# Inverses of pairs two and three of chunks on GpSimd, and a new cost model for the planner that orders the instructions

## The chip, the cores and the metric

One core of one Trainium2 chip. The metric is the time of one execution of the program on the device, in microseconds (us). Engines are named as the profile names them: PE (TensorE), DVE (VectorE), ACT (ScalarE), POOL (GpSimd), SP (SyncE, which here issues nearly all transfers).

## What is computed

A recurrent attention with a matrix state per head, over 768 positions, and then two feed-forward layers over the same 3072 tokens:

```python
batch, n_heads, seq, head_dim = (4, 8, 768, 40)
for t in range(S):
    y[:, :, t] = np.einsum('bhd,bhde->bhe', rt, state)
    Sa = np.einsum('bhde,bhe->bhd', state, at)
    state_decay = state * wt[:, :, None, :] - np.einsum('bhd,bhe->bhde', Sa, bt)
    state = state_decay + np.einsum('bhd,bhe->bhde', vt, kt)
x = y.transpose(0, 2, 1, 3).reshape(3072, 320)
h = x @ w_in;  g = h * np.tanh(log1p(exp(h)));  x = g @ w_out       # layer 1, d_ff 2048
h = x @ w_in2; g = h * np.cos(h);               out = g @ w_out2     # layer 2, d_ff 2048
```

## The kernel before

**Attention by chunks.** The 32 heads (batch times heads) are split into two halves of 16, the 768 positions into 24 pieces of 32. A *chunk* g = 0 to 47 is one piece of one half, g = 2c + half. For each chunk, `pre(g)` loads its inputs (line 565), scans the decays (571 to 577), scales a, k and b (585, 591), clears the other halves of the AM tile on POOL (memsets, 599), multiplies (PE, 608; transposes 641), masks the result (DVE, 618) and writes a 32 x 32 triangular matrix per head to `l_d` in DRAM (631, 632). `inverse(bt)` takes a *pair* of chunks, batch bt = chunks 2bt and 2bt+1: it loads their triangular matrices into XM (668), inverts the two 16 x 16 diagonal blocks of each by 14 rounds of a multiply (683) and an add (681), each depending on the one before, sets the diagonal by a memset (690), stores to `t_d` (694) and loads back as TT (698). `halves(bt)` then fills in the off-diagonal block (DVE 725, PE 720, DVE 728, PE 722, copy on ACT or DVE). `chain(g)` is the serial part: the right-hand side from the state (PE 791, copied by ACT, 797), its product with the inverse (805, for the first four chunks also 814), products 863 and 889, the new state (DVE 900, PE 933) and the output y (DVE 908). Chunk g needs the state of chunk g - 2.

**Feed-forward.** A block is 256 tokens, which are four chunks: block 0 needs chunks 0 to 3, block 1 chunks 4 to 7, and so on. `layer1(blk)` loads its input (1045 to 1047), splits it into a high and a low part (ACT 1050, DVE 1052), and multiplies (PE 993, 974) with nonlinear work between (ACT 1066, 1068, DVE 1071). `prep` brings the weights in 25 tiles for layer 1: load (458), convert (ACT 465, DVE 470 and 475, ACT or DVE 396/398), low half on POOL (505). `layer2` is similar with wider tiles (PE 1008 and 1025, POOL 1154).

**What sets the order.** All of this is put into tasks (`P.add(engine, duration, function, preds, ...)`), and `Plan.run` simulates the machine to list them: it takes, again and again, the engine and task that could start first, by the tasks' predicted durations, hops between engines, buffer rings, a port shared by DVE and POOL (`port=True`), and, for PE, a model of its clock (`HOT`, `DENSE` and each task's `cols`) and of the cost to change tile shapes. Among tasks that can start alike the lower `prio` goes first: chains about -1e4, `pre(g)` -5e3 + 10g, an inverse -5e3 + 10(g0 + 2) - 32, the weights of layer 1 -4921, the feed-forward blocks from 0 up. The functions are called in the order found, and that is the instruction order of every engine and of SP's queue; on the chip the engines run it as it stands, with semaphores. A transfer is a task of SP with a fixed time in the queue (0.5 to 2.0) and a fixed latency (`DMA_LAT` = 3.0, and up to 1.5 more) before its users may start. `TIE` seeds a change of up to 1% of each predicted duration.

Inverses: in `inverse`, `own = bt >= 3` decides whether the rounds run on POOL or, for the first three batches, on DVE.

Of the kernel before, what the change touches and what calls it, by code (L numbers as in the profile page):

```python
# [20 lines left out]
S = 768  # L21
# [34 lines left out]
class Task:  # L56
    __slots__ = ("eng", "dur", "fn", "preds", "acq", "rel", "aset", "lat", "prio", "end", "n_wait", "succ", "ready", "cols", "engs", "takes", "name", "durs", "bias", "ffn", "port", "mode", "soft", "pull", "mate")
# [24 lines left out]
HOT = 2750.0  # L82
# [6 lines left out]
SP_SAFE = 1.0  # L89
# [9 lines left out]
class Plan:  # L99
# [23 lines left out]
    def run(self):  # L123
# [15 lines left out]
        tick, hot, count, tick_no = TICK, False, 0.0, 0  # L139
        order = {id(t): i for i, t in enumerate(self.tasks)}  # L140
        while done < len(self.tasks):
# [67 lines left out]
            if e == "PE":  # L209
# [27 lines left out]
            for u in t.succ:  # L237
                for x in u.engs:
                    u.ready[x] = max(u.ready[x], free[e] + (HOP.get((e, x), 0.15) if t.lat is None else t.lat))
# [12 lines left out]
def body(ctx, tc, ins, out):  # L252
# [166 lines left out]
    EARLY = 1  # L419
# [4 lines left out]
    am_on, GLE = lambda g, d: ("DVE", 0.385), ("DVE",)  # L424
# [14 lines left out]
    def prep(layer, names, prio, after, stage, stage2, half):  # L439
# [5 lines left out]
        for kind, k, c0, n in jobs(layer):  # L445
# [32 lines left out]
            t3 = P.add("DVE", dve(n, 0.5), cvt1, preds=[t1], prio=prio, port=True)  # L478
# [75 lines left out]
    def pre(g):  # L554
# [38 lines left out]
        t_k = fifo("kb", P.add(*am_on(g, 0.65), kb_f(0), preds=[t_rp], acq=[("KB", k("KB"))], prio=pr, port=True))  # L593
        t_b = P.add(*am_on(g, 0.65), kb_f(1), preds=[t_k, t_a1], rel=[k("RP")] + ([] if g == 1 else [k("IN")]), prio=pr, port=True)
# [6 lines left out]
        t_z0 = P.add("POOL", 0.31, az_f(0), preds=[t_a1], prio=pr)  # L601
        t_z1 = P.add("POOL", 0.31, az_f(1), preds=[t_z0], prio=pr)
# [8 lines left out]
        t_g = P.add("PE", 0.46, g1, preds=[t_z1, t_b], acq=[("PA", k("G"), 4)], cols=925, prio=pr)  # L611
# [31 lines left out]
        def kbe(e):  # L643
            def f(eng):
                kp = pa(k("KT"))[64 * e:64 * e + 64, 0:4 * QP].rearrange("r (q x) -> r q x", x=QP)
                for p in range(2):
# [4 lines left out]
                    cols=500, prio=pr)  # L651
        KBe[g] = [P.add(KBE, 0.4 + 0.2 * e, kbe(e), preds=[t_t], rel=[k("KT")], prio=pr) for e in range(2)]

    def inverse(bt):
# [17 lines left out]
        own = bt >= 3  # L672
# [31 lines left out]
    def halves(bt, t):  # L704
# [22 lines left out]
        t = P.add("PE", HV_P, mm(0), preds=[t], acq=[("PA", k)], cols=180, prio=pr)  # L727
# [3 lines left out]
        t = P.add("PE", HV_P, mm(1), preds=[t], rel=[(k, "s")], cols=180, prio=pr)  # L731
# [41 lines left out]
    def chain(g):  # L773
# [34 lines left out]
        if g < DIRECT:  # L808
# [8 lines left out]
            def ztev(b, p):  # L817
                def f(eng):
# [4 lines left out]
            tz = P.add("PE", 0.3, ztm, preds=[t, ttld[g]], acq=[("PA", k("ZT0"), 2), ("PA", k("ZT1"), 2)], cols=230, prio=pr)  # L823
            zt = [P.add(EITHER, 0.27, ztev(b, p), preds=[tz, io[g][1]], rel=[k(f"ZT{b}")], bias=B_CH, prio=pr)
                  for b in range(2) for p in range(2)]
            t = P.add("PE", 0.3, zmm, preds=[t, tz, ttld[g]], acq=[("PA", k("Z"), 4)],
                      rel=[k("RS"), ("TT", bt)], cols=230, prio=pr)
        else:
            t = P.add("PE", 0.3, zmm, preds=[t, ttld[g]], acq=[("PA", k("Z"), 5)],
                      rel=[k("RS"), ("TT", bt)], cols=230, prio=pr)  # L830
# [8 lines left out]
            t2 = P.add("PE", 0.46, ztm, preds=[tz], acq=[("PA", k("ZT"), 2)], rel=[k("ZS")], cols=1000, prio=pr)  # L839
# [25 lines left out]
        r0 = P.add("PE", 0.46, rvz, preds=zt, acq=[("PA", k("V"), 2)], rel=[k("VR")], cols=925, prio=pr)  # L865
# [12 lines left out]
        for h in range(2):  # L878
            ve[h] = P.add("DVE", 0.41, rve(h), preds=[r0] + z[2 * h:2 * h + 2] + [ve[i] for i in range(h)], rel=[k("V")], prio=pr)
# [33 lines left out]
        f0 = P.add("PE", 0.56, fmm(0), preds=[ve[0]] + fpre[0], acq=[("PA", k("F0"))], cols=975, prio=pr)  # L913
        f1 = P.add("PE", 0.56, fmm(1), preds=[ve[1], f0] + fpre[1], acq=[("PA", k("F1"))], rel=[k("FL"), k("FR")], cols=975, prio=pr)
        mated("f", c, f0)
        sevs, yevs = [], []
        for h, ft in ((0, f0), (1, f1)):
            s = []
            if not last:
                s = [P.add("DVE", 0.315, sev(h, p), preds=[ft, io[nx][2]], prio=pr) for p in range(2)]  # L920
# [3 lines left out]
            yevs.append(P.add("DVE", 0.26, yev(h), preds=[ft] + s + yevs, acq=y_acq, rel=rel, prio=pr + 1))  # L924
        Sev[g] = sevs
        if not last:
            STev[g] = []
            for p in range(2):
# [13 lines left out]
                t = P.add("PE", 0.21, stm, preds=sevs, acq=[("PA", k(f"S{p}"), 2)], rel=[("SV", nx)], cols=185, prio=pr + 2)  # L942
# [19 lines left out]
    def outs(layer, blk, m, key, pr, preds, po, first, last):  # L962

        t = None
        for f in range(2):
            for j in range(2):
# [12 lines left out]
                t = P.add("PE", 0.44, mm, preds=list(preds) + [t], acq=acq, cols=840,  # L979
# [5 lines left out]
    def h_tasks(layer, key, m, pr, preds, xk):  # L985
        t = h_prev[0]
        for f in range(2):
            for part in range(2):
# [7 lines left out]
                t = P.add("PE", 0.48, mm, preds=list(preds) + [t], cols=880, acq=[("PH", (key, "h"))] if first else [],  # L996
# [4 lines left out]
    def h_wide(key, ft, pr, preds, xk, xh_t, xl_t):  # L1001

        t = h_prev[0]
        for part in range(2):
# [5 lines left out]
            t = P.add("PE", 0.91, mm, preds=list(preds) + [t], cols=1760, acq=[("PH", (key, "h"))] if part == 0 else [],  # L1010
# [4 lines left out]
    def outs_wide(ft, key, pr, preds, po):  # L1015
        t, tj = None, []
        for j in range(4):
# [9 lines left out]
            t = P.add("PE", 0.44, mm, preds=list(preds) + [t], acq=[("PO", (po, j))] if ft == 0 else [], cols=840,  # L1027
# [10 lines left out]
    def layer1(blk, wready):  # L1038
        pr0 = blk * 100
        xk = ("x1", blk)  # L1040
        xr = lambda: XR_t[P.at((xk, "xr"))]

        def ld():
# [143 lines left out]
    S_V = P.add("DVE", 2.0, setup_v, prio=-9e5)  # L1187
# [17 lines left out]
    wr1 = prep(1, ("w_in", "w_out"), -4921.0, [W1_AFTER()], ("RW", "H"), ("RL", "RA1"), half1)  # L1205
# [151 lines left out]
```

## Time and profile before

| | us |
|---|---|
| median of 3 runs | 1089.13 |
| lowest, highest | 1087.01, 1095.01 |
| span of the profiled execution | 1089.5 |
| PE busy in the span | 1006.6 (92%) |
| DVE busy | 742.0 (68%) |
| ACT busy | 544.0 (50%) |
| POOL busy | 429.8 (39%) |

The rows further down come from one execution taken by the hardware profiler. The span runs from its first to its last instruction; all starts are us from the span's start. A view by stretches gives for each stretch of time how long each engine was busy, the granted clock of PE (PEclk, 1.00 is full), and the load of the transfers. A view in order of time gives one line for an instruction or for several merged ones: its start, its length, the engine, the line of the kernel, and in square brackets what the engine was idle for before it. The shares over the whole span hide that the program has stages with different limits, so the stretches matter more than the totals.

### The profile page before, as it was taken

What the parts mean: (1) busy time and instruction counts of PE and PEld (TensorE: products, weight loads), DVE (VectorE), ACT (ScalarE), POOL (GpSimd) and SP (SyncE); (2) the same over time, 40 slices, a digit from 0 to 9 for tenths busy, and PEclk for the clock granted to TensorE, in tenths of its full rate; (3) what the DMA queues carried; (4) which work ended last, traced back from release to release, by engine and by line L of the source; (5) the groups of instructions that cost most, each with busy time, mean ns of one, the idle gap of its engine ahead of it and who ended that gap; (6) DMA issues with size and microseconds to landing.
All of it is one profiled execution on the core that took longest, in us unless ns stands there. A gap on an engine that the chain in (4) does not pass through costs nothing.

```text
span 1089.5 us, 36321 instructions
## 1 busy us (share of the span) xinstructions
PE 1006.6 (92%) x14888; PEld 926.8 (85%) x14888; DVE 742.0 (68%) x1652; ACT 544.0 (50%) x1338; POOL 429.8 (39%) x883
## 2 busy tenths in 40 slices
PE   1276899999999999999999999999999999999998
PEld 1265789888889988888998999999999999999997
DVE  8999888787577786678643797446655656565555
ACT  2345875655474655656564544434433434343433
POOL 4217646547344554355420242103333333333332
PEclk9999999999899999999999999999999999999999
DMA  6547665556445565455533543211100202010100
GB/s 206 149 134 231 173 166 145 154 143 170 108 137 160 145 168 127 122 152 151 137 90 100 173 152 96 85 42 35 42 13 1 54 1 54 1 40 1 25 1 25
DMA packets 109078, 111.88 MB, mean 103 GB/s; under 512 B 64112, under 2 KB 88688, under 8 KB 108912
## 3 DMA queue, kind: packets, MB, share of 16 engines
q1 hardware_dynamic: 108592, 109.24, 36.6%
q8 instruction: 117, 1.92, 0.7%
q14 instruction: 49, 0.40, 0.1%
q10 hardware_dynamic: 320, 0.33, 0.1%
HBM read 91.43 MB, written 18.09 MB: 101 GB/s over the span
## 4 chain that ended last, share of the span: by engine, by line
PE 75%; DVE 12%; DMA 5%; issue 4%; ACT 2%; SPq 1%; POOL 1%; DVEq 0%; POOLq 0%; ACTq 0%
PE bank L993 17%; PE bank L974 15%; PE bank L1008 14%; PE bank L1025 13%; PE bank L889 3%; PE bank L608 2%; DVE SV L900 2%; PE bank L863 1%; DMA VR<-in_vR_dram 1%; PE bank L641 1%; PE bank L837 1%; PE bank L791 1%; PE bank L933 1%; PE bank L805 1%; DVE AM L618 1%
## 5 line engine op out<-in xcount | busy, mean ns | idle before, releaser
L1154 POOL TENSOR_TENSOR GL<-H,GH 128x512 fp32r<-128x512 f32 x94 | 121.9, 1298 | 235.7 <-ACT GH L1152 219.1
L683 POOL TENSOR_TENSOR XT<-XM 64x14 f32<-64x14 f32 (+6 forms) x294 | 97.0, 330 | 174.5 <-DMA XM<-l_d 153.7
L396 ACT ACTIVATE FL<-bank 64x160 f32<-64x160 f32 (+1 forms) x375 | 101.4, 295 | 104.5 <-PE bank L641 51.6
L1145 ACT ACTIVATE T<-T,half_pi 128x512 f32<-128x512 f32 x96 | 69.5, 723 | 105.3 <-DVE T L1142 105.3
L1138 DVE TENSOR_SCALAR T<-bank 128x512 f32<-128x512 f32 x96 | 66.4, 692 | 76.7 <-PE bank L1008 63.2
L681 POOL TENSOR_TENSOR XM<-XM,XT 64x14 f32<-64x14 f32 (+6 forms) x294 | 106.0, 360 | 22.3
L1071 DVE TENSOR_TENSOR GL<-H,GH 128x512 fp32r<-128x512 f32 x96 | 70.1, 734 | 65.5 <-ACT GH L1068 63.7
L1147 DVE TENSOR_TENSOR H<-bank,T 128x512 f32<-128x512 f32 x96 | 66.1, 689 | 54.1 <-ACT T L1145 54.1
L1066 ACT ACTIVATE H<-bank 128x512 f32<-128x512 f32 x96 | 57.5, 598 | 87.9 <-PE bank L993 87.0
L1152 ACT ACTIVATE GH<-H 128x512 fp32r<-128x512 f32 x96 | 60.7, 632 | 73.9 <-DVE H L1147 73.9
L993 PE MATMUL bank<-XH,wih 128*128 128x256 f32 x448 | 95.4, 295 | 0.2 <-ACT GH L1068 0.2
L993 PE MATMUL bank<-XH,wil 128*128 128x256 f32 x448 | 89.7, 282 | 0.0
L993 PE MATMUL bank<-XL,wih 128*128 128x256 f32 x448 | 89.5, 282 | 0.0
L608 PE MATMUL bank<-AM,KB 104*64 104x64 f32 x768 | 37.0, 246 | 48.9 <-DVE KB L591 46.8
L618 DVE TENSOR_TENSOR AM<-bank,maskG 64x128 f32<-64x128 f32 x192 | 55.4, 288 | 35.8 <-PE bank L608 26.8
L608 PEld LDWEIGHTS bank<-AM,KB 104*64 104x64 f32 x768 | 30.5, 155 | 53.4 <-issue 35.4
L993 PEld LDWEIGHTS bank<-XH,wih 128*128 128x128 f32 x448 | 70.0, 192 | 2.2 <-ACT GH L1068 0.3
L993 PEld LDWEIGHTS bank<-XL,wih 128*128 128x128 f32 x448 | 69.7, 192 | 0.0
L993 PEld LDWEIGHTS bank<-XH,wil 128*128 128x128 f32 x448 | 69.6, 192 | 0.0
L1142 DVE SCALAR_TENSOR_TENSOR T<-T,bank 128x512 f32<-128x512 f32 x96 | 65.7, 685 | 2.4
L993 PE MATMUL bank<-XH,wix 128*128 128x256 f32 x224 | 67.1, 300 | 0.0
L900 DVE TENSOR_TENSOR SV<-bank,PE 40x160 f32<-40x160 f32 x184 | 58.9, 320 | 7.0 <-PE bank L889 3.8
(179 smaller groups left out, 2931.6 us busy)
## 6 DMA issues: line engine op xcount, KB each, us to landing
VR<-in_vR_dram SPq DMA_DIRECT2D x96, 160.0 KB
IN<-in_inT_dram SPq DMA_DIRECT2D x94, 161.4 KB
FR<-in_rI_dram SPq DMA_DIRECT2D x48, 180.0 KB
FR<-in_vF_dram SPq DMA_DIRECT2D x48, 144.0 KB
RA<-in_w_in_dram SPq DMA_DIRECT2D x12, 512.0 KB
RA<-in_w_out_dram SPq DMA_DIRECT2D x10, 512.0 KB
SV<-in_vS_dram SPq DMA_DIRECT2D x96, 52.0 KB
TMP<-in_w_in_dram SPq DMA_DIRECT2D x9, 512.0 KB
```

The lines of the kernel that those rows point to most:

```text
L396: A.activation(o, i, AF.Copy)
L608: PE.matmul(gp[c0:c0 + 64, q // 2], kb()[:, q].rearrange("p a t -> p (a t)"), am()[0:104, :, q], start=True, stop=True)
L681: IE.tensor_tensor(out=b[:, 0:i, i + 1:16], in0=b[:, 0:i, i + 1:16], in1=tv, op=ALU.add)
L683: IE.tensor_tensor(out=tv, in0=bc(b[:, i:i + 1, i + 1:16], (2 * n, i, w)), in1=bc(b[:, 0:i, i:i + 1], (2 * n, i, w)), op=ALU.mult)
L900: V.tensor_tensor(out=svn[r, p, :, 64 * h:64 * h + D], in0=fp[r, :, C:], in1=bc(pev(h)[r, :, C:C + 1], (40, 4, D)), op=ALU.mult)
L974: PE.matmul(o, l[:, f, tsl], r, start=(first and f == 0 and i == 0), stop=(last and f == 1 and i == 2))
L993: PE.matmul(hp[:, f], pss[i][0], pss[i][1], start=(i == 0), stop=(i == 7))
L1008: PE.matmul(bank[P.at((key, "h"))][:, 0:512], pss[i][0], pss[i][1], start=(i == 0), stop=(i == 7))
L1025: PE.matmul(o, l, r, start=(ft == 0 and i == 0), stop=(ft == NFF - 1 and i == 2))
L1071: gl = P.add(GLE, (dve(512),), lambda eng, Hv=Hv, key=key: EN[eng].tensor_tensor(out=GL_t[P.at((key, "gl"))], in0=Hv(), in1=GH_t[P.at((key ...
L1145: c = P.add("ACT", act(512, False, 1), lambda f=f, Tv=Tv: A.activation(Tv(f), Tv(f), AF.Sin, scale=-TWO_PI, bias=half_pi), preds=[b], aset ...
L1154: gl = P.add(*((VG, (pool(512), dve(512))) if final and quad == 7 else ("POOL", pool(512))), lambda eng, f=f, Hv=Hv, key=key: EN[eng].tens ...
```

## The change

Two kinds of edits. The first moves instructions from one engine to another: the rounds of the inverses of batches 1 and 2 (pairs two and three) go from DVE to POOL, so that only batch 0 is left on DVE. The others change numbers and rules of the planner, and so the order alone: a transfer now takes one of eight lanes in turn, waits in the queue until its lane is free (`ISSUE`, `LANES`), moves its data one after another with a fitted size and latency (`DMAS`), and its users may start 0.8 us (`LAND`) after that; PE's instructions are counted (`CODE`) and a block of 256 that was not fetched ahead in time costs waiting; durations and columns of many tasks are fitted anew; the clock thresholds follow the new columns; the weights of layer 1 go from priority -4921 (after `pre(7)`) to -4946 (after `pre(5)`); the input of block 0 (load, lines 1050 and 1052) goes from 0 to -9.94e3; the wait that a reused buffer cost an SP task, `SP_SAFE`, goes from 1.0 to 0, and the seed from 97 to 117.

```diff
-TIE = 97
+TIE = 117
-DENSE = 4400.0
-HOT = 2750.0
+DENSE = 5240.0
+HOT = 3277.0
-SP_SAFE = 1.0
+SP_SAFE = 0.0
+OWN, W1_PRIO = 1, -4946.0
+LAT_X = 0.0
+ISSUE, GAP_I, LANES, LAND = 0.36, 0.06, 8, 0.8
+DMAS = {"pre.ld": ((0.8, 2.0), (0.8, 2.0)), "pre.ldm": ((0.2, 1.0), (0.2, 1.0)), "inverse.ld": ((0.35, 1.15), (0.35, 1.15)),
...
+CODE = {"pre.g1": 32, "early.uu": 64, "early.<lambda>": 64, "halves.mm.f": 128, "chain.rhs": 64, "chain.zmm": 64,
...
+BLOCK, AHEAD_C, FETCH = 256, 78, 3.5
...
+                at, per = st, dur / t.code
+                for i in range(code, code + t.code):
+                    if i % BLOCK == 0 and i // BLOCK in fetched:
+                        w = max(0.0, fetched[i // BLOCK] - at)
+                        at, dur = at + w, dur + w
...
+            if t.dm:
+                cur = st
+                for size, l0 in t.dm:
+                    cur = max(cur, lanes[nd % LANES]) + ISSUE
+                    srv = max(srv, cur + l0) + size
+                    lanes[nd % LANES], nd = srv, nd + 1
+                    cur += GAP_I
+                dur = cur - st
...
-            t.end = free[e] + (0.2 if t.lat is None else t.lat)
+            t.end = srv + LAND if t.dm else free[e] + (0.2 if t.lat is None else t.lat)
...
-        own = bt >= 3
+        own = bt >= OWN
...
-                t = P.add("POOL" if own else "DVE", 0.1 + 0.0022 * i * (15 - i) if own else 0.165, step(i, add), preds=[t], lat=0.1 if own else 0.04, prio=pr, port=True)
+                t = P.add("POOL" if own else "DVE", 0.1 + 0.0022 * i * (15 - i) if own else 0.22, step(i, add), preds=[t], lat=0.1 if own else 0.04, prio=pr, port=True)
...
+        px = pr0 - 9.94e3 if blk < EARLY else pr0
...
-    wr1 = prep(1, ("w_in", "w_out"), -4921.0, [W1_AFTER()], ("RW", "H"), ("RL", "RA1"), half1)
+    wr1 = prep(1, ("w_in", "w_out"), W1_PRIO, [W1_AFTER()], ("RW", "H"), ("RL", "RA1"), half1)
```

Examples of the refitted numbers: line 585 from 0.385 to 0.43, line 591 from 0.385 to 0.342, line 618 from 0.27 to 0.298, line 900 from 0.315 to 0.34, line 908 from 0.26 to 0.22, line 797 from 0.29 to 0.328, `setup_v` from 2.0 to 4.0, and `cols` of PE tasks up by 2 to 67%, but for `chain.stm`, which goes down from 185 to 160.

## Rows read from the trace of the kernel before

**Rows 1.** Busy time by stretch: stretch, length, engines, granted clock (PEclk), transfers

```profile
core 0: us, PE busy (x) PEld busy (x) DVE busy (x) ACT busy (x) POOL busy (x), PEclk, DMA share, GB/s
0.00:115.00 115.00, 55.73 (x1325) 47.24 (x1326) 105.29 (x303) 47.19 (x133) 42.84 (x102) 1.00 0.62 177
...
140.00:600.00 460.00, 444.66 (x9946) 404.44 (x9943) 321.52 (x846) 268.86 (x797) 213.91 (x628) 0.99 0.53 140
...
800.00:1080.00 280.00, 280.00 (x1570) 253.53 (x1569) 162.96 (x250) 115.43 (x189) 99.95 (x77) 1.00 0.07 17
...
250.00:300.00 50.00, 46.45 (x994) 42.03 (x984) 31.72 (x84) 27.17 (x81) 26.19 (x84) 0.93 0.51 134
```

**Rows 2.** The same view, two stretches of 10 us within the head

```profile
50.00:60.00 10.00, 6.02 (x215) 4.99 (x215) 9.25 (x32) 3.15 (x12) 0.00 (x0) 1.00 0.24 74
...
70.00:80.00 10.00, 7.24 (x131) 6.29 (x132) 8.88 (x35) 4.68 (x14) 0.14 (x1) 1.00 0.60 152
```

**Rows 3.** DVE in order of time (start, length): batch 0, starts of 1 and 2

```profile
38.17 0.17 DVE L681 TENSOR_TENSOR XM<-XM,XT 64x26 f32<-64x26 f32 x1
...
43.70 0.17 DVE L681 TENSOR_TENSOR XM<-XM,XT 64x14 f32<-64x14 f32 x1
...
47.93 0.17 DVE L683 TENSOR_TENSOR XT<-XM 64x14 f32<-64x14 f32 x1
...
71.92 0.17 DVE L683 TENSOR_TENSOR XT<-XM 64x14 f32<-64x14 f32 x1
...
97.55 0.07 DVE L690 MEMSET XM<- 64x16 f32 x1
```

**Rows 4.** POOL in order of time: the first operation and the memset of batch 3

```profile
89.90 0.21 POOL L683 TENSOR_TENSOR XT<-XM 64x14 f32<-64x14 f32 x1 [3.65 <-DMA XM<-l_d]
...
102.72 0.12 POOL L690 MEMSET XM<- 64x16 f32 x1
```

**Rows 5.** ACT, PE, DVE in order of time: chunks 2, 3 to block 0

```profile
76.48 0.30 ACT L797 ACTIVATE RS<-bank 128x160 f32<-128x160 f32 x1
...
85.18 0.76 PE L814 MATMUL bank<-TT,RS 32*40 32x32 f32 x32 [0.40 <-ACT TT L396]
...
99.06 0.29 DVE L908 TENSOR_TENSOR Y<-bank,PE 104x128 f32<-104x128 f32 x1
...
111.07 0.84 ACT L1050 ACTIVATE XH<-XR 128x768 fp32r<-128x768 f32 x1 [2.56 <-DMA XR<-x_d]
...
113.78 0.95 DVE L1052 TENSOR_TENSOR XL<-XR,XH 128x768 fp32r<-128x768 f32 x1
...
114.73 0.78 PE L993 MATMUL bank<-XH,wih 128*128 128x256 f32 x2
```

**Rows 6.** POOL and DVE in order of time: operations that run side by side

```profile
45.91 1.82 POOL L505 TENSOR_TENSOR wol1a<-H,woh1a 128x512 fp32r<-128x512 f32 x1 [6.93 <-ACT woh1a L396]
...
46.61 1.40 DVE L585 TENSOR_TENSOR AM<-IN,PE 40x256 f32<-40x256 f32 x1
...
48.78 0.71 DVE L571 TENSOR_TENSOR_SCAN PE<-IN,D 104x264 f32<-104x264 f32 x1
...
99.21 0.85 POOL L681 TENSOR_TENSOR XM<-XM,XT 64x36 f32<-64x36 f32 x1
...
99.87 0.76 DVE L571 TENSOR_TENSOR_SCAN PE<-IN,D 104x264 f32<-104x264 f32 x1
```

**Rows 7.** SP's queue in order of time: loads of batches 1 and 2

```profile
41.94 0.78 SPq L668 DMA_DIRECT2D XM<-l_d  x2
...
62.24 0.78 SPq L668 DMA_DIRECT2D XM<-l_d  x2
```

**Rows 8.** The chain that ended last, in order of time: a weight tile

```profile
91.53 4.38 DMA RL<-in_w_in_dram
```

**Rows 9.** ACT in order of time: the input of block 2

```profile
211.44 0.84 ACT L1050 ACTIVATE XH<-XR 128x768 fp32r<-128x768 f32 x1 [1.83 <-DMA XR<-x_d]
```

More of the change, by code (lines that the diff above doesn't have):

```diff
@@ L56 @@
 class Task:
-    __slots__ = ("eng", "dur", "fn", "preds", "acq", "rel", "aset", "lat", "prio", "end", "n_wait", "succ", "ready", "cols", "engs", "takes", "name", "durs", "bias", "ffn", "port", "mode", "soft", "pull", "mate")
+    __slots__ = ("eng", "dur", "fn", "preds", "acq", "rel", "aset", "lat", "prio", "end", "n_wait", "succ", "ready", "cols", "engs", "takes", "name", "durs", "bias", "ffn", "port", "mode", "soft", "pull", "mate", "code", "dm")
     def __init__(self, eng, dur, fn, preds=(), acq=(), rel=(), aset=None, lat=None, prio=0.0, cols=0.0, bias=BIAS, port=False):
@@ L76, in __init__ @@
         self.mate = None
-TIE = 97
+        self.code = 64 if self.name == "chain.ztm" and dur < 0.4 else CODE.get(self.name, 8)
+        self.dm = DMAS.get(self.name) if eng == "SP" else None
+        if self.dm and "prep" in self.name and dur < 0.5:
+            self.dm = ((0.9, 1.6),)
+TIE = 117
 TICK = 10.24 / 3
-DENSE = 4400.0
-HOT = 2750.0
+DENSE = 5240.0
+HOT = 3277.0
 MODE = {"pre.g1": "128x64", "chain.rvz": "128x64", "chain.fmm.f": "128x64", "chain.rhs": "128x32",
@@ L88 @@
 WAIT = 8.0
-SP_SAFE = 1.0
+SP_SAFE = 0.0
[3 more added lines that the diff above has]
+DMAS = {"pre.ld": ((0.8, 2.0), (0.8, 2.0)), "pre.ldm": ((0.2, 1.0), (0.2, 1.0)), "inverse.ld": ((0.35, 1.15), (0.35, 1.15)),
+        "inverse.st": ((0.3, 1.0), (0.3, 1.0)), "inverse.<lambda>": ((0.6, 1.45),),
+        "load_step.f1": ((1.14, 1.6), (0.8, 1.3)), "load_step.f2": ((0.8, 2.0), (0.8, 2.0)),
+        "load_step.f3": ((0.24, 1.2), (0.24, 1.2)), "prep.<lambda>": ((1.8, 1.6),), "chain.yst": ((0.46, 1.0), (0.46, 1.0)),
+        "layer1.ld": ((0.5, 1.45),) * 3, "layer1.<lambda>": ((0.35, 1.3),),
+        "layer2.ld": ((0.3, 1.3),) * 4, "layer2.store": ((0.24, 1.3),) * 2}
+CODE = {"pre.g1": 32, "early.uu": 64, "early.<lambda>": 64, "halves.mm.f": 128, "chain.rhs": 64, "chain.zmm": 64,
+        "chain.rvz": 32, "chain.fmm.f": 32, "chain.sel": 20, "outs.mm": 6, "outs_wide.mm": 6}
+BLOCK, AHEAD_C, FETCH = 256, 78, 3.5
 def mode_cost(a, b):
@@ L139, in run @@
         tick, hot, count, tick_no = TICK, False, 0.0, 0
+        code, fetched = 0, {0: 0.0, 1: 0.0}
+        self.starved = 0.0
+        lanes, nd, srv = [0.0] * LANES, 0, 0.0
         order = {id(t): i for i, t in enumerate(self.tasks)}
@@ L225, in run @@
                     count += t.cols
-                recent.append((st + dur, t.cols))
+                at, per = st, dur / t.code
[3 more added lines that the diff above has]
+                        at, dur = at + w, dur + w
+                        self.starved += w
+                    if (i + AHEAD_C) % BLOCK == 0:
+                        b = (i + AHEAD_C) // BLOCK + 1
+                        fetched[b] = max(at, fetched.get(b - 1, 0.0) - FETCH / 2) + FETCH
+                    at += per
+                code += t.code
+                recent.append((st + dur, t.cols))
+            if t.dm:
[6 more added lines that the diff above has]
+                dur = cur - st
             free[e] = st + dur + sw
@@ L238, in run @@
                 for x in u.engs:
-                    u.ready[x] = max(u.ready[x], free[e] + (HOP.get((e, x), 0.15) if t.lat is None else t.lat))
+                    u.ready[x] = max(u.ready[x], t.end if t.dm else free[e] + (HOP.get((e, x), 0.15) if t.lat is None else t.lat) + (LAT_X if x == "PE" != e and not u.ffn else 0.0))
                 u.n_wait -= 1
@@ L878, in chain @@
         for h in range(2):
-            ve[h] = P.add("DVE", 0.41, rve(h), preds=[r0] + z[2 * h:2 * h + 2] + [ve[i] for i in range(h)], rel=[k("V")], prio=pr)
+            ve[h] = P.add("DVE", 0.43, rve(h), preds=[r0] + z[2 * h:2 * h + 2] + [ve[i] for i in range(h)], rel=[k("V")], prio=pr)
         yb, yc = divmod(c, 2)
@@ L919, in chain @@
             if not last:
-                s = [P.add("DVE", 0.315, sev(h, p), preds=[ft, io[nx][2]], prio=pr) for p in range(2)]
+                s = [P.add("DVE", 0.34, sev(h, p), preds=[ft, io[nx][2]], prio=pr) for p in range(2)]
             sevs += s
@@ L995, in h_tasks @@
                 first = f == 0 and part == 0
-                t = P.add("PE", 0.48, mm, preds=list(preds) + [t], cols=880, acq=[("PH", (key, "h"))] if first else [],
+                t = P.add("PE", 0.48, mm, preds=list(preds) + [t], cols=1024, acq=[("PH", (key, "h"))] if first else [],
                           rel=[(xk, "xh"), (xk, "xl")] if (m == 7 and f == 1 and part == 1) else [], prio=pr)
@@ L1008, in mm @@
                     PE.matmul(bank[P.at((key, "h"))][:, 0:512], pss[i][0], pss[i][1], start=(i == 0), stop=(i == 7))
-            t = P.add("PE", 0.91, mm, preds=list(preds) + [t], cols=1760, acq=[("PH", (key, "h"))] if part == 0 else [],
+            t = P.add("PE", 0.91, mm, preds=list(preds) + [t], cols=2048, acq=[("PH", (key, "h"))] if part == 0 else [],
                       rel=[(xk, "xh"), (xk, "xl")] if (ft == NFF - 1 and part == 1) else [], prio=pr)
```

56 lines of the change are left out of this document (28 added, 28 removed).

## The prediction

> **What bounds the kernel now.** Read the stretches by engine first, then the head by engine in order of time.
>
> From 140 to 600 us TensorE is busy 444.66 of 460, and from 800 to 1080 all of 280 [rows 1]; nothing but less TensorE work or a higher clock shortens that. In the first 115 us it is busy 55.73, so 59.3 are idle, and there VectorE is busy 105.29, 92% [rows 1]. Between 50 and 80 us GpSimd does almost nothing (0.00 and 0.14 in the two stretches shown) while VectorE is at 9.25 and 8.88 of 10 [rows 2]. So the program has two parts: a head that VectorE sets, which ends when the first feed-forward matmul (line 993) starts at 114.73 [rows 5], and a rest that TensorE sets. If the head is shorter and the rest stays as dense, the end moves by the same amount.
>
> **The change part by part.**
>
> *Inverses.* With `own = bt >= 1` the operations of lines 681 and 683 of batches 1 and 2 (pairs two and three) and a memset each go from VectorE to GpSimd: 2 x 28 = 56 steps of the inverses. What a step holds of VectorE is best read from batch 0, which ran almost alone: its 25 steps from the one that starts at 38.17 to the one that starts at 43.70 [rows 3] have 24 pitches in 5.53 us, 0.23 each with the gap. Of interleaved steps the latency is partly hidden by other work, so I take 0.225: 56 x 0.225 = 12.6 us of VectorE time that leaves the head, all of it before 97.6 [rows 3].
>
> Is that time on the path? Batch 1 starts on VectorE at 47.93 and batch 2 at 71.92, right behind it, and its memset is at 97.55 [rows 3]: 24.0 and 25.6 us per batch, because the steps take turns with everything else. On GpSimd batch 3 took from 89.90 to 102.72, 12.8 us, at a busy VectorE [rows 4]. Batch 1's load is issued at 41.94 and batch 2's at 62.24 [rows 7], each long before VectorE is through with it. With some 4 us to land (the tile on the chain took 4.38 [rows 8]; an estimate) GpSimd could finish batch 1 at about 46 + 13 = 59 instead of 71.9, batch 2 at about 79 instead of 97.6. Who waits for batch 1: chunks 2 and 3. Their right-hand side is copied by 76.48 + 0.30 = 76.8, and the product with the inverse starts at 85.18 [rows 5]: 8.4 us in which only the inverse is missing. Their last y is at 99.06, and it releases the input of the first feed-forward block [rows 5]. So the direct path gives 8.4 us, and the VectorE budget of the same stretch 12.6; since VectorE has hardly a gap before and behind that bubble, I take 12.6 and keep 8.4 as what is sure of it.
>
> *What it costs GpSimd.* 2 x 12.8 = 25.6 us, laid on an engine idle for most of 40 to 90 [rows 2]: nothing, while that cover lasts. Behind these steps in GpSimd's order stand the memsets of line 599, which the next pair's first matmuls (line 608) need, and the low halves of the weights (line 505). A step of 12.8 / 28 = 0.46 ahead of a memset delays it by that much; only a batch that waits for its own load would hold them for longer.
>
> *Contention.* An operation of VectorE can stand still beside one of GpSimd: line 585 at 46.61 takes 1.40 and ends only when line 505 (45.91 + 1.82 = 47.73) is over [rows 6]. Nothing here shows a step of batch 1 or 2 on GpSimd; the nearest rows are batch 3's. There the step at 99.21 stretched to 0.85 itself, while the scan that VectorE ran behind it took 0.76 against 0.71 at 48.78 [rows 6]. Bounds: nothing, and a whole pitch per step, 56 x 0.46 = 25.8. I take the scan's 0.05: 56 x 0.05 = 2.8 us.
>
> The Trainium skill (SBUF — State Buffer, "Who interferes with whom") says that a VectorE instruction with two SBUF inputs and a GpSimd instruction that reads SBUF exclude each other, the later one blocked for the whole instruction. The 1.40 agrees; which engine pays is by that page a matter of who starts first, and by it every step could cost VectorE its full time, which is the third rival below.
>
> *Block 0's input.* Its load, line 1050 and line 1052 get a priority behind the chains of chunks 0 to 5 alone. Line 1050 ends at 111.07 + 0.84 = 111.91, line 1052 starts at 113.78 [rows 5] behind other VectorE work: 1.9 us to gain. The load can gain more, or nothing; nothing is taken.
>
> *Weights of layer 1 earlier* (-4946 for -4921): they pass the preparation of chunks 6 and 7. The work is the same. The first block needs them sooner if it starts sooner, so I cost this at nothing; what hides it is the VectorE time just freed. Without that, see the second rival.
>
> *All other edits* (durations, columns, thresholds, seed, code fetch, eight lanes, landing slack, safety of SP) change no instruction, only the order, on SP's queue too. What order can give in the stretch to 600 us is bounded by its 15.3 us of idle TensorE and the 250 to 300 stretch at a granted clock of 0.93, 0.07 x 50 = 3.5 us [rows 1]: -18.8 at best. At worst it loses as much again. TensorE is 97% busy there, so I take 0, and about 8 either way for the range.
>
> **The sum.** 12.6 - 2.8 + 1.9 = 11.7 us off a span of 1089.5, 1077.8. The median of the runs before, 1089.13, is 0.4 below that span; so 1077.
>
> **Rivals.**
>
> 1. *Given back at block 2, about 1086.* Block 2's input reached ScalarE only at 211.44, after a wait of 1.83 for its load [rows 9]: the feed-forward part had caught up with the chains there. If the freed VectorE time goes into weights and not into chunks 4 to 11, the first block is early and later ones are not, and TensorE idles around 200 what it gained at 115. For it: the earlier weights do just that. Against: fewer VectorE steps help the chains too. With the 8.4 us kept only in part (0 to 6): 1083 to 1089; "no change" is this at its worst. Chance 0.31.
>
> 2. *Weight conversions stand ahead of their transfers: slower.* VectorE and ScalarE run in a fixed order. Where the plan puts a conversion ahead of the preparation of chunks 6 and 7 and its tile is late, both wait. A tile stood 4.38 us on the chain once [rows 8]. The 11.7 us are gone at 2.7 such waits; at six, 26.3 us, the time is 1089.5 - 11.7 + 26.3 = 1104. For it: the earlier the conversions stand, the nearer they are to their transfers, and 2.7 is not many among 25 tiles. Against: the plan now adds a slack to each landing, and more queueing ahead of it. Chance 0.08.
>
> 3. *The excluded pair: slower.* If VectorE pays for each step of GpSimd, 25.8 - 12.6 - 1.9 = 11.3, so 1101. It decides from 14.5 / 56 = 0.26 us per step on. Against: 0.05 beside batch 3 [rows 6]. Chance 0.05.
>
> 4. *The order itself is better in the dense part.* Half of the 18.8 [rows 1] on top: 1077 - 9 = 1068. Against: nothing there waits long for data. Chance 0.13.
>
> **How the numbers follow.** The forecast has 0.43, with a range of its own from 1071 (order +, load of block 0 faster) to 1082 (only 8.4 of the 12.6, less 2.8, plus 1.9). Range: down to 1066, past rival 4's centre, and up to 1091, past rival 1 and a part of the order's 8 to the worse; below lie about 0.05, above 0.15. About 1% (10.9 us) is what a measurement of this kernel can tell from no change; faster means below 1078. Faster: three quarters of the forecast's 0.43, 0.13 of rival 4 and a little of rival 1, 0.05, together 0.50. Slower: rivals 2 and 3, 0.13, and 0.01 of the forecast. The rest, 0.36, is within 1%.
>
> **What would show it.** In the profile after: lines 681 and 683 on VectorE only 28 times; on GpSimd batch 1 from about 46 to 59; the product of chunks 2 and 3 with the inverse near 77; first line 993 at 101 to 106; VectorE's busy time to that point about 12 us less. If line 993 starts early and the end does not move, the input of blocks 2 and 3 (line 1050) has not moved from 211 and rival 1 holds. Scans and line 585 longer beside GpSimd's steps mean rival 3; VectorE or ScalarE idle on weight tiles before 115 rival 2; less than 15.3 us idle in the same dense stretch rival 4. What would make me wrong at the root is a head whose end some transfer sets, so that VectorE's free time only becomes idle time.

## The result and the profile after

| | before | after |
|---|---|---|
| median of the runs measured together (4 and 4), us | 1089.57 | 1076.12 |
| lowest, highest | 1087.01, 1095.01 | 1073.77, 1082.62 |
| ratio, with 95% interval | | 0.989 (0.9848 to 0.9932) |
| span of the profiled execution | 1089.5 | 1072.0 |

13.5 us by these medians; the forecast was 1077. The size came out as predicted. Where the time went did not, and most of what follows is about that. One profile is one draw (the kernel before alone ran from 1079.33 to 1093.24 us in 31 later runs), so sizes are taken from ratios and places from profiles. Ratios and their intervals leave out executions more than 1.5% above the fastest of a kernel and are not quotients of the medians shown, which are over all its runs.

A line of before has the same code as the line 38 further on in after (39 from line 1040 on): 681, 683, 993, 1045, 1050, 1052 are now 719, 721, 1031, 1084, 1089, 1091.

First the stretches by engine, as in [rows 1]: stretch, length, busy time and instructions of each engine, granted clock, share of the transfer engines, GB/s.

```profile
core 0: us, PE busy (x) PEld busy (x) DVE busy (x) ACT busy (x) POOL busy (x), PEclk, DMA share, GB/s
0.00:115.00 115.00, 56.19 (x1416) 47.49 (x1416) 95.58 (x252) 50.98 (x144) 66.00 (x160) 0.85 0.65 182
140.00:600.00 460.00, 451.00 (x10048) 413.21 (x10046) 326.90 (x856) 273.83 (x811) 216.98 (x648) 0.99 0.54 145
```

VectorE is relieved: 95.58 in the head for 105.29, GpSimd has 66.00 for 42.84. TensorE's busy time in the head is as it was, 56.19 for 55.73, but with 91 matmuls more (1416 for 1325). In the dense stretch it idles 9.0 us for 15.3.

Busy time over the whole span, the page's first part, after:

```profile
PE 995.8 (93%) x14888; PEld 919.2 (86%) x14888; DVE 730.1 (68%) x1597; ACT 542.7 (51%) x1335; POOL 450.7 (42%) x941
```

TensorE runs the same 14888 instructions in 995.8 us, and before it was busy 1006.6. Idle time is the span less that: 82.9 before, 76.2 after. So of 17.5 us between the two profiled spans 6.7 are idle time and 10.8 are shorter busy time.

Now the head in order of time, each row a start, a length, engine, line, operation and what it waited for in brackets; these rows answer to [rows 5].

```profile
62.42 0.74 PE L843 MATMUL bank<-RS,TT 32*32 32x40 f32 x29 [3.03 <-issue]
65.02 0.87 DVE L911 TENSOR_TENSOR FR<-bank,maskR 64x256 f32<-64x256 f32 x2 [4.99 <-PE bank L901]
...
75.65 0.30 ACT L835 ACTIVATE RS<-bank 128x160 f32<-128x160 f32 x1
...
82.72 0.76 PE L852 MATMUL bank<-TT,RS 32*40 32x32 f32 x32
...
99.01 0.29 DVE L946 TENSOR_TENSOR Y<-bank,PE 104x128 f32<-104x128 f32 x1
100.56 0.28 SPq L991 DMA_DIRECT2D x_d<-Y  x1
...
104.63 0.39 SPq L1084 DMA_DIRECT2D XR<-x_d  x1
...
112.32 0.84 ACT L1089 ACTIVATE XH<-XR 128x768 fp32r<-128x768 f32 x1
...
114.96 0.28 DVE L656 TENSOR_TENSOR AM<-bank,maskG 64x128 f32<-64x128 f32 x1
115.25 0.42 DVE L911 TENSOR_TENSOR FR<-bank,maskR 64x256 f32<-64x256 f32 x1
115.71 0.96 DVE L1091 TENSOR_TENSOR XL<-XR,XH 128x768 fp32r<-128x768 f32 x1
116.69 0.51 PE L1031 MATMUL bank<-XH,wih 128*128 128x256 f32 x2
```

The product of chunks 2 and 3 with the inverse starts at 82.72, 2.5 earlier than before's 85.18; the last y of block 0 is at 99.01 for 99.06; the first feed-forward matmul is at 116.69, **later** than 114.73. The head did not become shorter. And yet layer 1 ended earlier. The first and last start of its first matmul group, before and after (minimum, median and longest of one in ns, then first and last start):

```profile
L993 PE MATMUL bank<-XH,wih x448: 276/281/580, 114.7 to 786.7; 128*128 128x256 f32 x150
...
L1031 PE MATMUL bank<-XH,wih x448: 276/281/415, 116.7 to 770.9; 128*128 128x256 f32 x150
```

The start is 2.0 later, the last one 15.8 earlier. What remains to the end is 301.1 us after and 302.8 before: layer 2 has hardly changed. So from its first to its last start this group takes 654.2 us where it took 671.9, and that has to be explained.

### The profile page after: what moved, and what is told of

Same layout as the page of the kernel before. It is cut to its first block, busy times and chain, and to the rows that moved or that the text cites. A ratio compares the mean times of both kernels' runs of the same rounds, so it can differ in the third digit from the quotient of the medians.

```text
span 1072.0 us, 36318 instructions
## 1 busy us (share of the span) xinstructions
PE 995.8 (93%) x14888; PEld 919.2 (86%) x14888; DVE 730.1 (68%) x1597; ACT 542.7 (51%) x1335; POOL 450.7 (42%) x941
## 4 chain that ended last, share of the span: by engine, by line
PE 80%; DVE 9%; DMA 4%; issue 3%; ACT 2%; POOL 0%; SPq 0%; DVEq 0%; ACTq 0%; POOLq 0%
PE bank L1012 17%; PE bank L1031 17%; PE bank L1046 14%; PE bank L1063 13%; PE bank L927 4%; PE bank L901 2%; PE bank L646 2%; PE bank L875 2%; PE bank L679 2%; PE bank L843 2%; PE bank L760 1%; PE bank L758 1%; PE bank L829 1%; DVE SV L938 1%; PE bank L971 1%
## 5 line engine op out<-in xcount | busy, mean ns | idle before, releaser
L721 POOL TENSOR_TENSOR XT<-XM 64x14 f32<-64x14 f32 (+6 forms) x322 | 112.3, 349 | 182.1 <-DMA XM<-l_d 159.1
L434 ACT ACTIVATE FL<-bank 40x160 f32<-40x160 f32 (+1 forms) x375 | 101.4, 295 | 87.8 <-PE bank L679 55.0
L719 POOL TENSOR_TENSOR XM<-XM,XT 64x14 f32<-64x14 f32 (+6 forms) x322 | 114.9, 357 | 24.8
```

The source lines that it names most:

```text
L434: A.activation(o, i, AF.Copy)
L719: IE.tensor_tensor(out=b[:, 0:i, i + 1:16], in0=b[:, 0:i, i + 1:16], in1=tv, op=ALU.add)
L721: IE.tensor_tensor(out=tv, in0=bc(b[:, i:i + 1, i + 1:16], (2 * n, i, w)), in1=bc(b[:, 0:i, i:i + 1], (2 * n, i, w)), op=ALU.mult)
```

## Experiments

**The two halves of the change apart.** The diff does two things: it moves 56 steps of the inverses to another engine, and it changes the order of everything. Two kernels separate them. In both the planner still runs on its own assumption, so that the order is kept, and only the engine that gets the steps is changed.

*The move alone, in the old order* (label e1_move_alone, on the kernel before):

```
-        IE = G if own else V
+        IE = G if bt >= 1 else V
```

> The kernel before with its order kept on TensorE, ScalarE and SyncE; only the rounds of the inverses of batches 1 and 2 are issued on GpSimd, at the places that they had. If the head's VectorE time was the gain (the prediction's theory), 56 x 0.225 = 12.6 us leave VectorE and the time falls by 8 to 12, to about 1078 to 1082, with the first feed-forward matmul (line 993) near 103 to 107. If the gain came from the new order of the dense part, it stays within 3 us of 1089, and line 993 starts within 4 us of 114.7.

Measured: 1081.30 us against 1086.03 of the kernel before, run beside it, ratio 0.9953 (0.9924 to 0.9981). That is 5.1 us at 1086, less than the 8 to 12 of the head theory and more than the 3 of the other.

*The new order alone, with the move taken back* (label e2_move_back, on the kernel after):

```
-        IE = G if own else V
+        IE = G if bt >= 3 else V
```

> The changed kernel with its order kept; the rounds of batches 1 and 2 are issued on VectorE again, at the places that they have on GpSimd. Head theory: VectorE carries 12.6 us more before the first feed-forward matmul and the time goes back to about 1086 to 1089. Order theory: at most 4 us more, 1074 to 1080.

Measured: 1082.25, ratio 0.9968 (0.9939 to 0.9996), between the two ranges. Beside the 0.989 of after, the move is worth 0.8% in the new order, some 8.5 us, and the order without the move 0.3%, 3.5 us. The 0.989 rests on four runs (0.9848 to 0.9932), so a difference to it is uncertain by about 0.5% (an estimate from the two intervals).

The same group of matmuls in e1_move_alone, then in e2_move_back, first and last start:

```profile
L993 PE MATMUL bank<-XH,wih x448: 276/280/582, 108.3 to 776.1; 128*128 128x256 f32 x150
```

```profile
L1031 PE MATMUL bank<-XH,wih x448: 276/281/582, 123.8 to 779.9; 128*128 128x256 f32 x150
```

and the first part of their pages, in the same sequence:

```profile
PE 1002.8 (93%) x14888; PEld 924.0 (86%) x14888; DVE 729.9 (68%) x1594; ACT 544.2 (50%) x1338; POOL 448.0 (42%) x941
```

```profile
PE 998.5 (92%) x14888; PEld 921.3 (85%) x14888; DVE 741.3 (69%) x1655; ACT 543.1 (50%) x1335; POOL 427.3 (40%) x883
```

With the spans 1079.1 (e1_move_alone) and 1081.1 (e2_move_back) this makes a square of four:

| step | first matmul of layer 1 | from first to last | TensorE idle | TensorE busy |
|---|---|---|---|---|
| move, old order (before to e1) | -6.4 | -4.2 | -6.6 | -3.8 |
| move, new order (e2 to after) | -7.1 | -2.0 | -6.4 | -2.7 |
| order, no move (before to e2) | +9.0 | -15.8 | -0.3 | -8.1 |
| order, with the move (e1 to after) | +8.4 | -13.6 | -0.1 | -7.0 |

These are four single executions. Their spans differ by more than the ratios say (10.4 us for the move in the old order, where the ratio gives 5.1), so the table shows where a part works and not how much it is worth.

The two halves work in different places, and the signs are the same in both rows. The move brings the head forward by 6.4 to 7.1 us and takes as much idle time from TensorE over the whole span. The order makes the head longer by some 9 us, and then saves 14 to 16 within layer 1. Their sum in the head is nearly nothing, which is why 116.69 stands beside 114.73.

The same four executions by stretches, each with the head and then layer 1 from its first to its last start (before, e1_move_alone, e2_move_back, after):

```profile
0.00:114.73 114.73, 55.46 (x1325) 46.97 (x1325) 105.20 (x302) 46.93 (x132) 42.57 (x102) 1.00 0.62 177
114.73:786.67 671.94, 652.78 (x11888) 609.30 (x11886) 462.31 (x1082) 375.37 (x1008) 282.67 (x702) 0.99 0.47 128
...
0.00:108.29 108.29, 50.92 (x1325) 43.37 (x1325) 93.97 (x244) 46.91 (x132) 61.85 (x160) 0.85 0.65 186
108.29:776.08 667.79, 653.36 (x11887) 610.07 (x11886) 461.42 (x1082) 375.56 (x1008) 281.55 (x702) 0.98 0.47 129
...
0.00:123.77 123.77, 58.62 (x1449) 49.59 (x1449) 109.43 (x313) 52.41 (x148) 43.21 (x102) 0.83 0.60 172
123.77:779.94 656.17, 643.20 (x11776) 602.84 (x11774) 457.97 (x1076) 369.63 (x989) 280.83 (x702) 0.99 0.47 129
...
0.00:116.69 116.69, 57.40 (x1448) 48.56 (x1448) 97.22 (x255) 52.49 (x148) 66.00 (x160) 0.85 0.65 182
116.69:770.88 654.19, 641.73 (x11777) 601.79 (x11774) 458.88 (x1076) 369.14 (x989) 281.61 (x702) 0.99 0.48 130
```

What the order saves in layer 1 is for the most part busy time: 9.6 of the 15.8 us without the move, 11.7 of the 13.6 with it; the rest is idling. Not all of it is saved. The new order runs some 124 matmuls of the attention before layer 1 begins, so the head's busy time is 3.1 and 6.5 us larger. The granted clock explains a part in one row only: by the clock records of the traces TensorE ran at the lower of its two levels (1.2 GHz) for 13.7 us of layer 1 in before and in e2_move_back alike, but for 24.5 in e1_move_alone and 10.2 in after, which at half speed is up to 7 of the 11.7 us (an estimate).

**Why the head gives 6.4 for 12.** VectorE's busy time fell by 12.1 us in the move alone (742.0 to 729.9, 58 instructions fewer) and by 11.2 in the new order (741.3 to 730.1, again 58). The path got 6.4 and 7.1. To compare with [rows 3] and [rows 5], four more rows of before: the memset that ends batch 1, and from SP's queue the store of batch 2's inverse, the first of the two last stores of block 0's y, and the load of block 0:

```profile
71.82 0.07 DVE L690 MEMSET XM<- 64x16 f32 x1
...
98.65 0.95 SPq L694 DMA_DIRECT2D t_d<-XM  x2
...
100.45 0.31 SPq L952 DMA_DIRECT2D x_d<-Y  x1
...
104.30 0.38 SPq L1045 DMA_DIRECT2D XR<-x_d  x1
```

In e1_move_alone the path in order of time, with the memsets that end batches 1 and 2 on GpSimd:

```profile
64.67 0.13 POOL L690 MEMSET XM<- 64x16 f32 x1
...
77.86 0.76 PE L814 MATMUL bank<-TT,RS 32*40 32x32 f32 x32 [0.40 <-ACT TT L396]
...
91.23 0.29 DVE L908 TENSOR_TENSOR Y<-bank,PE 104x128 f32<-104x128 f32 x1
...
93.26 0.12 POOL L690 MEMSET XM<- 64x16 f32 x1
93.41 0.78 SPq L694 DMA_DIRECT2D t_d<-XM  x2
...
95.09 0.32 SPq L952 DMA_DIRECT2D x_d<-Y  x1
...
98.60 0.38 SPq L1045 DMA_DIRECT2D XR<-x_d  x1
...
104.63 0.84 ACT L1050 ACTIVATE XH<-XR 128x768 fp32r<-128x768 f32 x1 [3.88 <-DMA XR<-x_d]
...
108.29 0.78 PE L993 MATMUL bank<-XH,wih 128*128 128x256 f32 x2
```

Batch 1's inverse is done 7.2 us earlier (64.67 for 71.82), and the product that needs it 7.3 (77.86 for 85.18). From there to the last y it takes 13.4 us for 13.9, so y is 7.8 earlier (91.23 for 99.06): the half of the freed time that is batch 2's gains some 0.5 us on this stretch. Then 2.4 of the 7.8 are lost, of which 1.0 comes back by line 993. In this order batch 2 takes 28.4 us on GpSimd (64.88 to 93.26, for 25.6 on VectorE before), and the store of its inverse stands in SP's queue ahead of the stores of y. So y, done at 91.52, leaves at 95.09, 5.4 earlier than before; its load is issued 5.7 earlier, line 1050 and line 993 start 6.4 earlier. The longest wait of SP's queue from 85 to 100 us, and two of VectorE between 40 and 115 us, in the same kernel (line that waits, what for: total, times, longest):

```profile
SPq L694 <- POOL XM L690: 2.6, 1, 2.6
...
DVE TA L725 <- DMA TT<-t_d: 4.0, 2, 2.3
DVE H L470 <- ACT H L465: 3.7, 3, 1.9
```

Before, the last two were 0.2 and 0.6. So VectorE waits 7.7 us there for 0.8, but all of it except 0.35 us falls after the last y of block 0 (at 99.39, 106.06, 110.56 and 112.50): it shows where freed time turned into idle time, not what holds the head. What holds it is batch 1's inverse, and then SP's queue behind batch 2's.

**Which part of the new order?** First the seed, which the change also moved from 97 to 117 (e3_seed97, on after):

```
-TIE = 117
+TIE = 97
```

> The changed kernel with the planner's seed at 97, as before: other ties, the same model. If the model is what gains, the time stays within 5 us of 1076. If the seed was lucky, it is 8 us or more above, 1084 to 1092.

Measured: 1098.29, ratio 1.0065 (1.0028 to 1.0102): the new cost model and the move, with the old seed, are slower than before.

Then the transfer model (e4_old_transfers, on after): the old fixed times in SP's queue are used again, everything else stays.

```
-        self.dm = DMAS.get(self.name) if eng == "SP" else None
+        self.dm = None
...
-SP_SAFE = 0.0
+SP_SAFE = 1.0
```

> The changed kernel planned with the old model of transfers (fixed time in the queue and fixed latency, 1.0 us of safety for a reused buffer); all else as changed. If lanes, fitted transfers and slack are what gains, the time goes back to 1084 to 1090. If the fitted durations, columns and the count of fetched code gain, it stays at 1074 to 1080.

Measured: 1086.77, ratio 1.0011 (0.998 to 1.0042). Taken alone this says that the eight lanes and the fitted transfers are worth 1.2%. But a seed that is worth 1.8% had just been seen, so neither run says what its edit does. What has to be asked is how far kernels differ that differ in the seed alone.

**Seeds.** Two more for the kernel after (e5_after_seed1, e6_after_seed33), two for the kernel before (e7_before_seed117, e8_before_seed1), each with the one line `TIE = ...` changed.

> The changed kernel with the planner's seed at 1. If the new model of costs is what makes the order better, the ratio to before stays at 0.985 to 0.995. If an order is one draw among many and seed 117 a good one, the ratio falls anywhere from 0.985 to 1.015, and with seed 97 (1.0065) and seed 33 most lie above 0.995.

> The changed kernel with the planner's seed at 33. Model theory: 0.985 to 0.995 of before. Draw theory: anywhere from 0.985 to 1.015, and not near that of seed 1 or 97 by more than chance.

> The kernel before with the planner's seed at 117. Draw theory: the seed before was chosen too, so another one is slower, 1.003 to 1.02 of before. Model theory: within 0.5% of before, 0.995 to 1.005, since it is the model and not the seed that sets the time.

> The kernel before with the planner's seed at 1. Draw theory: 1.003 to 1.02 of before. Model theory: 0.995 to 1.005. If the mean over the seeds tried is lower with the new model than with the old one by 0.5% or more, the model helps beside the seed.

And the old transfers of e4_old_transfers again, with seeds 1 and 33 (e9_old_tr_seed1, e10_old_tr_seed33):

> As the run with the old model of transfers, with the planner's seed at 1 (with the new transfers seed 1 measured 0.999 of before, seed 33 0.9954, seed 117 0.989; the old transfers at seed 117 1.0011). If the model of transfers makes better orders, this is again about 0.01 above its partner: 1.004 to 1.015. If the 1.0011 was only a worse draw than the chosen 117, it lies within 0.005 of 0.999.

> The same with the seed at 33. Transfers theory: 1.0 to 1.011 of before. Draw theory: within 0.005 of 0.9954.

Last, two seeds of after that were picked beforehand because the planner's own reckoning ends early for them, as a test whether that reckoning ranks orders (e11_after_seed304, e12_after_seed215):

> The changed kernel with a seed whose plan ends, by the planner's own reckoning, as early as that of seed 117, the earliest of 150 seeds looked at. If the planner's reckoning ranks the orders rightly, the ratio is that of seed 117 again, 0.984 to 0.993. If 117 was luck that the planner can't see, it lies with the seeds that were not picked (mean of 1, 33 and 97: 1.0003), 0.995 to 1.007.

> The same with another of the seeds whose plans end earliest. Ranking theory: 0.984 to 0.993. Luck theory: 0.995 to 1.007.

All of them together. "First" is the start of the first matmul of layer 1, "idle" what TensorE idles of the 460 us from 140 to 600, both from the one profiled execution. That one can lie far from the median: for e11 it took 1072.58.

| kernel | seed | first | idle | median us | ratio (95%) |
|---|---|---|---|---|---|
| before | 97 | 114.7 | 15.3 | | 1 |
| before, e7 | 117 | 138.1 | 17.7 | 1095.74 | 1.0097 (1.0061 to 1.0133) |
| before, e8 | 1 | 129.5 | 23.1 | 1104.95 | 1.0169 (1.0113 to 1.0225) |
| after | 117 | 116.7 | 9.0 | 1076.12 | 0.989 (0.9848 to 0.9932) |
| after, e3 | 97 | | | 1098.29 | 1.0065 (1.0028 to 1.0102) |
| after, e5 | 1 | 117.1 | 13.0 | 1083.92 | 0.999 (0.9961 to 1.0019) |
| after, e6 | 33 | 116.6 | 5.5 | 1081.27 | 0.9954 (0.9924 to 0.9984) |
| after, e11 | 304 | 122.4 | 7.4 | 1083.46 | 0.9979 (0.9945 to 1.0013) |
| after, e12 | 215 | 122.3 | 7.6 | 1074.81 | 0.991 (0.9882 to 0.9938) |
| after, old transfers, e4 | 117 | 111.9 | 19.9 | 1086.77 | 1.0011 (0.998 to 1.0042) |
| after, old transfers, e9 | 1 | 110.7 | 8.9 | 1074.79 | 0.992 (0.9893 to 0.9947) |
| after, old transfers, e10 | 33 | 108.8 | 10.1 | 1085.05 | 0.9993 (0.9958 to 1.0028) |

What follows:

- *A seed is worth as much as the change.* It alters each predicted duration by up to 1% and no instruction; it moves the time from 0.989 to 1.0065 in the kernel after, and by 1.7% in the kernel before.
- *The two seeds that before and after carry are each the best of those tried for their kernel.* The seeds that nobody picked give 1.0097 and 1.0169 for before (mean 1.0133), and 1.0065, 0.999, 0.9954 for after (mean 1.0003). By these the change as a whole is worth about 1.3%, near the 1.1% of the pair itself; by the spread of so few draws that difference has a standard error of about half a per cent, and with two draws against three its 95% interval reaches zero (both are estimates).
- *The transfer model is not shown to help.* New and old, seed by seed: 0.989 and 1.0011, 0.999 and 0.992, 0.9954 and 0.9993. It wins twice and loses once; the means are 0.9945 and 0.9975. The 0.992 lies below what either theory had for it.
- *Whether the planner's reckoning ranks orders stays open.* Of the two picked by it one is good (0.991), the other (0.9979) lies amid the unpicked. With seed 117, which it ranks first too, the three that it favours have a mean of 0.9926, the three others 1.0003, and the two groups overlap.
- *The start of layer 1 does not foretell the end; the idle time in the dense stretch does better.* Over the kernels with both numbers and e1 and e2 (10.5 and 10.1 idle), 13 in all, the ratio correlates with the idle time at 0.84 and with the first matmul at 0.59; the span of the very execution that was profiled correlates with them at 0.92 and 0.43. TensorE's time at the lower clock in the same stretch goes with the idle time (0 us in e6 and e11, 41.0 in e8; it correlates with the span at 0.90), so which of the two the time follows is not shown. The old transfers start early (108.8 to 111.9) and end anywhere from 0.992 to 1.0011.

The dense stretch of the slowest kernel, e8_before_seed1, and then of one of the fastest, e12_after_seed215 (columns as in the stretches above):

```profile
140.00:600.00 460.00, 436.93 (x9719) 396.12 (x9718) 320.27 (x838) 263.62 (x788) 213.66 (x632) 0.96 0.52 138
```

```profile
140.00:600.00 460.00, 452.42 (x10084) 413.14 (x10081) 328.83 (x863) 275.06 (x817) 222.65 (x653) 1.00 0.53 144
```

In the same 460 us the second gets through 365 more matmuls, busy 15.5 us longer and at a granted clock of 1.00, where the first idles more and is granted 0.96 on the mean. No kernel that was run is better than the kernel after by a difference that its interval can tell.

## Why the prediction was right or wrong, step by step

**VectorE time that leaves: 12.6.** Right as a quantity: 12.1 and 11.2 us of VectorE's busy time went with 58 instructions. Line 721 runs 14 times on VectorE, 719 as often, 28 together, as said. Line 721 by engine, with count, shortest, median and longest in ns, and first and last start, after:

```profile
L721 POOL TENSOR_TENSOR XT<-XM x322: 205/274/2974, 44.3 to 552.3; 64x14 f32<-64x14 f32 x23, 64x36 f32<-64x36 f32 x23, 64x50 f32<-64x50 f32 x23, 64x56 f32<-64x56 f32 x23
L721 DVE TENSOR_TENSOR XT<-XM x14: 174/204/1168, 38.3 to 45.2; 64x14 f32<-64x14 f32 x2, 64x26 f32<-64x26 f32 x2, 64x36 f32<-64x36 f32 x2, 64x44 f32<-64x44 f32 x2
```

**All of it on the path: wrong, 6.4 to 7.1.** The step that failed is "is that time on the path?", answered with a yes for the whole. VectorE at 92% was read as a bound that would stay the bound, and its 12.6 us were taken in place of the direct path's 8.4. The direct path was nearly right: the product with the inverse came 7.3 us earlier in the old order and 6.2 in the new one (82.72 for 88.96 in e2_move_back). Batch 2's half of the freed time fell behind that product and gained the path some 0.5 us. Then, in the old order, a transfer set the end of the head, which the prediction had named as what would make it wrong: the stores of block 0's y stood in SP's queue behind that of batch 2's inverse, which waited 2.6 us for GpSimd.

**GpSimd's batches.** Batch 1 was said to run from 46 to 59, batch 2 to 79. GpSimd in order of time, after:

```profile
44.30 0.21 POOL L721 TENSOR_TENSOR XT<-XM 64x14 f32<-64x14 f32 x1 [4.91 <-DMA XM<-l_d]
...
51.33 2.97 POOL L721 TENSOR_TENSOR XT<-XM 64x56 f32<-64x56 f32 x1
...
61.30 0.12 POOL L728 MEMSET XM<- 64x16 f32 x1
...
66.26 0.21 POOL L721 TENSOR_TENSOR XT<-XM 64x14 f32<-64x14 f32 x1 [2.03 <-DMA XM<-l_d]
...
78.23 0.12 POOL L728 MEMSET XM<- 64x16 f32 x1
79.98 1.26 POOL L543 TENSOR_TENSOR wix<-H,wix 64x512 fp32r<-64x512 f32 x1
```

17.0 us and 12.0: right for the second, 4 more for the first, in which one step stood for 2.97. In e1_move_alone, where the steps keep the places that they had, it was 20.1 and 28.4. The product of chunks 2 and 3, forecast near 77, was at 77.86 in the old order and at 82.72 in the new one.

**Contention, -2.8: between nothing and that.** The 58 operations that left VectorE took 12.3 us there in before and 14.1 in e2_move_back, by their own lengths, and its busy time fell by 12.1 and 11.2. A cost of the steps on GpSimd to VectorE's other work would show as a smaller fall: 0.2 us is left over in the old order, 2.9 in the new one. Its other operations, compared one by one, took 2.6 us less in e1_move_alone than before and 1.8 more in after than in e2_move_back, nearly all of it in a few long stalls that come and go. Rival 3, the excluded pair, priced at 0.46 a step, is refuted: 25.8 us are nowhere. What does stretch are the steps themselves, on GpSimd (2.97 above), and VectorE beside the weights' low halves: VectorE in order of time, after, the operation that ran beside line 543 at 79.98 and a later one of the same line:

```profile
80.03 1.49 DVE L629 TENSOR_TENSOR KB<-IN,RP 104x256 f32<-104x256 f32 x1
...
109.61 0.41 DVE L629 TENSOR_TENSOR KB<-IN,RP 104x256 f32<-104x256 f32 x1
```

The first takes 1.49, the other 0.41. That kind stood in [rows 6] already (1.40 beside line 505), and it came with the weights, not with the inverses. The rule of the Trainium skill (SBUF — State Buffer, "Who interferes with whom"), by which a two-input operation of VectorE and GpSimd's reading shut each other out for a whole instruction, fits these long stalls; for the 56 short steps the measured sum decides, and by it VectorE paid at most 2.9 us.

**Block 0's input, 1.9: not gained.** Line 1091 starts at 115.71, 2.55 after line 1089 is through (112.32 + 0.84); before it was 1.9. The load is issued 4.07 after the last store of y (100.56 to 104.63), behind loads of later chunks and of weights on SP's queue; before it was 3.5. The changed priority bought neither the place in the queue nor the one on VectorE: operations of the chains, of a weight and of `pre` stand ahead of line 1091.

**All other edits, 0: wrong for this seed.** "TensorE is 97% busy there, so I take 0" was the reasoning. The order is worth -3.5 us by e2_move_back and, with the move, -6.9 (0.989 to 0.9953), in two opposite parts: +9 in the head, -14 to -16 in layer 1. The bound of 18.8 to the better held in size, but not for its reason: it counted idle time and clock, and most of the gain in layer 1 is busy time. The "as much to the worse" held too, as e3_seed97 and the seeds of before show.

**The sum.** 11.7 forecast, 12.0 measured (1.1% of 1089.57). Term by term: the move 5.1 to 8.5 for 9.8 (12.6 - 2.8), line 1052 nothing for 1.9, the order 3.5 to 6.9 for 0. The prediction also set a median against the span of a profile, but an execution takes 1.8 us longer than its span (1073.77 for 1072.0 after), so the profile of before shows one of about 1091.3, above its median (an estimate). The right total came by luck, from one term too large and one left at nothing.

**Rivals.** Rival 1 had line 993 early, block 2's input unmoved and the end unmoved. The input did stay (210.63 for 211.44), but the start was late and the end moved, by what came after: the last block's input was at 652.58 for 670.19. Rival 2, conversions waiting for transfers, is not seen as a loss: the last tile of layer 1's low halves starts at 172.46 for 185.90. Rival 4, a better order in the dense part, came with its sign (9.0 us idle for 15.3), but the sign does not tell the order from the move: e1_move_alone, in the old order, has 10.5, and e2_move_back 10.1. Its price was 9 on top of the move; the order brought 14 to 16 in layer 1 and gave 9 of them back in the head, so it stands beside a smaller move, not on top of the forecast.

**What stays open.** Which of the refitted durations, columns, code count, weight priority and landing slack shortens layer 1 by 14 to 16 us was not settled: each was to be judged by kernels that also redraw the order, and a redraw is worth as much. Nor is it settled where the 8 us of TensorE's busy time went; with the move a part can be the clock, without it not. Another part shows in one group, line 933 before and line 971 after, 368 matmuls each (busy, mean ns, idle before; before, then after):

```profile
L933 PE MATMUL bank<-ident,SV 40*104 40x40 f32 x368 | 27.8, 232 | 4.6 <-DVE Y L908 2.6 <-DVE SV L900 1.2 <-DVE AM L618 0.2
```

```profile
L971 PE MATMUL bank<-ident,SV 40*104 40x40 f32 x368 | 23.2, 225 | 3.4 <-DVE Y L946 2.2 <-ACT RS L835 1.0
```

4.6 us for the same work; in e2_move_back, which has the order alone, it is 24.1, but in e1_move_alone, which has the old order, 25.9, so not all of it is the order. Overlap with the neighbours in TensorE's order is a likely reason, but that is argued, not shown.

## What to carry to other kernels

An engine at 92% in a serial stretch is a bound only until the next one: before counting all the time that leaves it, ask which part of it lies ahead of the wait that is on the path (here batch 1's half, which gave about what the direct path had forecast) and what comes behind it (here a store in SP's queue). When an edit moves work and also lets a planner draw a new order, build the two mixed kernels (new engine in the old order, old engine in the new one) first: they cost two runs and gave the sizes of the two parts. A planner's draw is worth about 1% by itself, so an edit to its costs is judged over several seeds on both sides, not by one pair.

## What the runs showed of the hardware

- The page's granted clock for the head can't be compared between profiles: before it reads 1.00 from 0 to 115 us [rows 1], after 0.85, for nearly the same busy time (55.73 and 56.19). The first clock record of before is at 117.9 us, that of after at 69.8; what lies ahead of it reads as 1.00.
- TensorE's waits named "issue" are not small: 3.03 us in front of one group of 32 x 32 matmuls (62.42 above), and VectorE then waited 4.99 for what came behind it.
- 56 short two-input operations on GpSimd beside a busy VectorE cost it at most 2.9 us (0.2 by busy time in one order, 2.9 in the other), while one 64 x 512 operation on GpSimd (79.98) had VectorE's neighbour stand for about 1.1 us more than its 0.41.
